# Six-block attention and two gated layers on one core: how the second block's probabilities are normalised and transposed, how two biases and merged weight bits are formed, and an order that knows of an exclusion between two engines

## The chip, the cores and the metric

The kernel runs on one core of one Trainium2 chip. The number is device microseconds from the start to the end of one execution. An engine is named as the profile names it: PE (TensorE, matmuls; PEld is its weight load), DVE (VectorE), ACT (ScalarE), POOL (GpSimd), SP (SyncE, which here issues most DMAs). PSUM is the memory that PE writes, in 8 banks of 128 x 512 fp32 numbers; SBUF is the working memory.

## The reference

```python
# q, k, v: 4 x 8 x 576 x 64, fp32
scores = scale * q @ k^T                       # per batch and head, 576 x 576
kth = the 32nd largest of each row
scores = where(scores >= kth, scores, -1e9)
attn = exp(scores - max) / (sum + 1e-9)
x = (attn @ v) laid out as 2304 x 512
h = x @ w_in ;  x = (h * sigmoid(h)) @ w_out   # w_in 512 x 2048, w_out 2048 x 512
out = (((x @ w1) * (x @ w2)) @ w3) @ w_out2    # w1, w2 512 x 1024, w3 1024 x 1024, w_out2 1024 x 512
```

## The kernel before

The weights arrive as 64-bit floats, read as pairs of 32-bit words. The 2304 tokens are worked in six blocks of 384 (`BLOCKS`), each three tiles of 128 rows for each of 8 heads. While the dense layers of block j run on PE (`mlp`), the attention of block j + 1 runs on the other engines and in PE's gaps. Block 0's attention has no dense layer to run beside; in its place the product of w3 and w_out2 is formed (`fold_steps`). The dense layers of block 0 run together with the conversion of the 48 pieces of w_in, w_out, w1 and w2 (`conv_step`), which later blocks read back from DRAM.

**Scores and top-k** (`plan_scores`, `plan_topk`). Two tiles make a pair; a block has 12 pairs. For each tile DVE finds the 32 largest of 576 scores with four MAX8 and three MATCH_REPLACE8. The eight-number results go into `tops`, which has a zero column in front and one behind, so that one subtraction of two strided columns (`bias`) gives both `nb` numbers of both tiles: minus the largest and minus the 32nd. ACT then masks (`mask`, with the 32nd) and takes the exponential (`ex`, with the largest), summing it. `recip` forms `rc`, one over the sum.

**Normalising and transposing** (`norm`, `plan_av`). In blocks 0 and 1 (`NATIVE`) the identity times `rc` is written as `dg` (by ACT for the first four pairs, by POOL after that), and an fp32 matmul of the unnormalised `e` with `dg` transposes and normalises at once, in five chunks of each tile. In blocks 2 to 5 POOL multiplies `e` itself by `rc`, and PE's transpose with the identity follows.

**Conversion of a weight piece.** `convert_load` brings 128 x 512 pairs into `raw`. `convert_scale`: ACT scales the high words into `t`; the low words are reduced to their top three bits, by ACT (`low` is the bias of that step) or, for even pieces from the eighth on (`LOWV`), by a DVE shift, in both cases back into `raw`; POOL clamps `t`. `convert_bits`: for the conversion a DVE SCALAR_TENSOR_TENSOR shifts `t` left by three and merges the low bits (`w<-t,raw`); for the fold (`MERGE`) DVE shifts and POOL adds. Then ACT rounds `w` into the first half of `wt` and POOL subtracts for the second.

**Order.** Every instruction is first recorded (`Recorder`); `schedule` then runs through them with costs of its own (`Op.cost`) and sets the order of each engine's queue, which is fixed in the program. Every recorded instruction has the line of the call in `emit`, so rows are told apart by their tiles. All PSUM tiles share one pool of 8 buffers (`bank`).

## Time and profile before

| | |
|---|---|
| median of 3 runs | 1153.53 us (1153.19 to 1156.3) |
| the profiled execution | 1153.59 us, its span from first to last instruction 1151.8 us |
| busy over the span | PE 95%, PEld 87%, DVE 81%, ACT 74%, POOL 65% |
| last matmul of the fold | starts at 142.2 us |
| first matmul of block 0's dense layers | starts at 172.7 us |
| merges of the 48 pieces | start from 148.2 to 368.8 us |

A profile row gives the engine, the operation, its output and input tiles, the shapes, a count, the busy time and the mean of one. Idle time stands behind the second bar, with what ended it. L328 is the line in `emit` from which all recorded instructions are issued.

### The profile page before, as it was taken

The page shows a single profiled execution, that of the slowest core. Times are in us where ns is not written, and L with a number is a line of the kernel's source. Part 1 is how long each engine was busy: PE and PEld are TensorE (multiplying, and loading weights), DVE is VectorE, ACT ScalarE, POOL GpSimd, SP SyncE. Part 2 cuts the span into 40 slices and gives each one's busy share as a digit, 9 for nine tenths or more (in the row PEclk, how much of TensorE's full clock was granted, in tenths as well). Part 3 has the DMA queues.
Part 4 walks back from the last instruction along what each step waited for, and adds up shares of the span by engine and source line. Part 5 has one row for each costly group of instructions (what it writes and reads, how often), then busy time and mean ns, then how long its engine had stood idle before and what let it go on. Part 6 is the DMA issues. An engine that isn't in the chain of part 4 may idle for free.

```text
span 1151.8 us, 19674 instructions
## 1 busy us (share of the span) xinstructions
PE 1097.8 (95%) x6216; PEld 998.5 (87%) x6216; DVE 927.7 (81%) x1990; ACT 854.6 (74%) x1911; POOL 744.0 (65%) x767
## 2 busy tenths in 40 slices
PE   4889987989999999999999999999999999999998
PEld 3555566979898999999999998999999999999997
DVE  7999899999979899999999997898899999501100
ACT  6988699879887688888888877877878788642221
POOL 4678368887876476777777866776766577542221
PEclk9999988999999999999999999999999999999999
DMA  8886278898989677675888667898766766348840
GB/s 250 282 271 197 92 256 281 311 310 317 313 267 316 201 237 235 216 240 183 276 268 276 216 225 242 268 321 291 241 212 230 249 217 221 127 154 259 253 152 28
DMA packets 127879, 273.54 MB, mean 237 GB/s; under 512 B 40480, under 2 KB 65056, under 8 KB 127776
## 3 DMA queue, kind: packets, MB, share of 16 engines
q1 hardware_dynamic: 119712, 245.02, 65.7%
q10 hardware_dynamic: 8064, 27.27, 6.0%
q8 instruction: 50, 0.82, 0.3%
q14 instruction: 53, 0.43, 0.1%
HBM read 216.14 MB, written 56.10 MB: 236 GB/s over the span
## 4 chain that ended last, share of the span: by engine, by line
PE 58%; DVE 21%; ACT 8%; POOL 6%; issue 5%; DMA 2%; ACTq 0%; SPq 0%; POOLq 0%; DVEq 0%
PE bank L328 58%; DVE tops L328 9%; DVE wk L328 7%; DVE w L328 2%; ACT e L328 2%; POOL wt L328 2%; POOL gl L328 1%; DMA kk<-k 1%; DVE gf L328 1%; ACT st L328 1%; POOL t L328 1%; DVE nb L328 1%; ACT wt L328 1%; ACT t L328 1%; DMA scr<-wt 1%
## 5 line engine op out<-in xcount | busy, mean ns | idle before, releaser
L328 DVE MAX8 tops<-wk 128x8 f32<-128x576 f32 x432 | 320.5, 753 | 5.7
L328 POOL TENSOR_TENSOR gl<-gf,gh 128x384 fp32r<-128x384 f32 x144 | 148.8, 1033 | 162.8 <-ACT gh L328 161.7
L328 PE MATMUL bank<-gh,wt 128*128 128x384 f32 x768 | 225.9, 344 | 7.3 <-ACT gh L328 7.1
L328 PE MATMUL bank<-xh,wt 128*128 128x384 f32 x768 | 223.2, 341 | 0.3 <-ACT st L328 0.2
L328 PE MATMUL bank<-x2h,wt 128*128 128x384 f32 x768 | 219.7, 341 | 0.1
L328 DVE MATCH_REPLACE8 wk<-tops,wk 128x576 f32<-128x576 f32 x288 | 213.2, 741 | 0.0
L328 PE MATMUL bank<-kk,qs 128*128 128x288 f32 x640 | 149.5, 320 | 16.0 <-ACT kk L328 13.2
L328 ACT ACTIVATE st<-bank 128x288 f32<-128x288 f32 (+1 forms) x320 | 129.0, 410 | 38.0 <-PE bank L328 33.4
L328 POOL TENSOR_TENSOR pl<-pf,ph 128x384 fp32r<-128x384 f32 x128 | 129.7, 1021 | 37.9 <-ACT ph L328 36.1
L328 PEld LDWEIGHTS bank<-gh,wt 128*128 128x128 f32 x768 | 141.2, 189 | 9.0 <-ACT gh L328 8.3
L328 PEld LDWEIGHTS bank<-kk,qs 128*128 128x128 f32 x640 | 116.0, 194 | 34.7 <-issue 16.5
L328 PEld LDWEIGHTS bank<-xh,wt 128*128 128x128 f32 x768 | 141.6, 189 | 2.4 <-issue 0.8
L328 PEld LDWEIGHTS bank<-x2h,wt 128*128 128x128 f32 x768 | 140.7, 188 | 2.7 <-DVE gf L328 0.5
L328 PE MATMUL bank<-gl,wt 128*128 128x384 f32 x384 | 131.3, 342 | 3.8 <-POOL gl L328 3.4
L328 DVE MAX8 tops<-st 128x8 f32<-128x576 f32 x144 | 107.6, 751 | 32.4 <-ACT st L328 31.9
L328 PE MATMUL bank<-x2l,wt 128*128 128x384 f32 x384 | 129.0, 337 | 0.5 <-POOL x2l L328 0.4
L328 PE MATMUL bank<-xl,wt 128*128 128x384 f32 x384 | 129.3, 337 | 0.1
L328 ACT ACTIVATE e<-st,nb 128x576 f32<-128x576 f32 x144 | 107.7, 777 | 19.5 <-DVE nb L328 18.2
L328 ACT CAST gh<-gf 128x384 fp32r<-128x384 f32 x144 | 74.0, 514 | 60.4 <-DVE gf L328 58.1
L328 ACT ACTIVATE e<-e,nb 128x576 f32<-128x576 f32 x144 | 111.3, 775 | 0.5 <-POOL wt L328 0.5
L328 DVE SCALAR_TENSOR_TENSOR gf<-th,bank 128x384 f32<-128x384 f32 x96 | 52.3, 545 | 68.8 <-ACT th L328 66.9
L328 DVE MATCH_REPLACE8 wk<-tops,st 128x576 f32<-128x576 f32 x144 | 106.5, 741 | 0.0
(80 smaller groups left out, 2374.5 us busy)
## 6 DMA issues: line engine op xcount, KB each, us to landing
wt<-scr SPq DMA_DIRECT2D x240, 512.0 KB, 4.2
scr<-wt ACTq DMA_DIRECT2D x48, 512.0 KB, 5.7
k<-kk SPq DMA_DIRECT2D x32, 576.0 KB, 4.5
kk<-k SPq DMA_DIRECT2D x32, 576.0 KB, 5.2
raw<-in_w_dram SPq DMA_DIRECT2D x24, 512.0 KB, 5.5
kr<-in_kT_dram SPq DMA_DIRECT2D x32, 288.0 KB, 5.0
raw<-in_w3T_dram SPq DMA_DIRECT2D x16, 512.0 KB, 5.0
raw<-in_w_in_dram SPq DMA_DIRECT2D x16, 512.0 KB, 5.2
```

The costliest lines, as they stand in the source:

```text
L328: o.call(*[real_ap(x) for x in o.args], **{k: real_ap(x) for k, x in o.kw.items()})
```

## The change

The change has four parts. Block 1 (`NATIVE` but not `DIAG`) lets POOL multiply `e` by `rc` and transposes with the identity; block 0 keeps `dg`. The biases are formed by two TENSOR_REDUCE with one input each, in place of one subtraction with two inputs, and `tops` becomes a tile `top` of a pool. For the 28 of 48 pieces whose low bits ACT forms, ACT writes them to a PSUM bank (`LOWP`), so that the merge reads one input from PSUM. And `schedule` holds a DVE instruction that `port` marks as sharing back while a POOL instruction runs by its costs, and the other way round; if POOL is busy for more than `AVOID` ns, a ready DVE instruction that does not share goes first.

```diff
+AVOID = 60
+DIAG = lambda j: j == 0
+LOWP = lambda n: n >= 0
...
+    def port(self):
+        if self.engine != "vector" or self.name in ("max", "match_replace", "tensor_reduce", "reciprocal"):
+            return False
+        return not in_bank(self.ins)
...
             if self.name == "tensor_scalar":
-                t = 850 if src.dtype == I16 else max(360, n * 1.14 + 45)
+                t = 740 if src.dtype == I16 else max(360, n * 1.14 + 45)
...
+            late = 0.
+            if o.shares and busy > t + AVOID:
+                aside = [n]
+                while ready[e] and ops[ready[e][0]].shares:
+                    aside.append(heapq.heappop(ready[e]))
+                n = heapq.heappop(ready[e]) if ready[e] else aside.pop(0)
+                for x in aside:
+                    heapq.heappush(ready[e], x)
+                o = ops[n]
+            if o.shares:
+                late = max(0., busy - t)
+                held = t + late + o.hold
+            elif e == "gpsimd":
+                late = max(0., held - t)
+                busy = t + late + o.hold
...
         if LOWV(n):
-            nc.vector.tensor_scalar(r[:, :, 0], r[:, :, 0], 29, None, op0=ALU.logical_shift_right)
+            u = r[:, :, 0]
+            nc.vector.tensor_scalar(u, u, 29, None, op0=ALU.logical_shift_right)
         else:
-            nc.scalar.activation(out=r[:, :, 0].bitcast(I32), in_=r[:, :, 0], func=ACTF.Identity,
+            u = bank("low") if LOWP(n) else r[:, :, 0].bitcast(FP32)
+            nc.scalar.activation(out=u.bitcast(I32), in_=r[:, :, 0], func=ACTF.Identity,
                                  bias=low, scale=2.0 ** -29 * (1.0 - 2.0 ** -16))
...
-            nc.vector.scalar_tensor_tensor(out=w.bitcast(U32), in0=t.bitcast(U32), scalar=3, in1=r[:, :, 0],
+            nc.vector.scalar_tensor_tensor(out=w.bitcast(U32), in0=t.bitcast(U32), scalar=3, in1=u,
...
         def bias():
             t = st["top"]
-            nc.vector.tensor_sub(out=st["nb"][:, 0:m], in0=t[:, 0:m, TOPK:TOPK + 2], in1=t[:, 0:m, 1:TOPK + 1:TOPK - 1])
+            nc.vector.tensor_reduce(out=t[:, 0:m, TOPK:TOPK + 2], in_=t[:, 0:m, 0:TOPK:TOPK - 1].unsqueeze(3), axis=AX, op=ALU.add, negate=True)
+            nc.vector.tensor_reduce(out=st["nb"][:, 0:m], in_=t[:, 0:m, TOPK - 1:TOPK + 1], axis=AX, op=ALU.add)
...
-            if NATIVE(j):
+            if NATIVE(j) and not DIAG(j):
+                x = p = e[:, 0:S]
+            elif NATIVE(j):
...
-                        nc.tensor.matmul(ps[0:kn, i * 128:(i + 1) * 128], lhsT=p[:, kc * 128:kc * 128 + kn],
-                                         rhs=st["d"][:, i * 128:(i + 1) * 128], start=True, stop=True)
+                        if DIAG(j):
+                            nc.tensor.matmul(ps[0:kn, i * 128:(i + 1) * 128], lhsT=p[:, kc * 128:kc * 128 + kn],
+                                             rhs=st["d"][:, i * 128:(i + 1) * 128], start=True, stop=True)
+                        else:
+                            nc.tensor.transpose(ps[0:kn, i * 128:(i + 1) * 128], p[:, kc * 128:kc * 128 + kn], ident)
```

The queue of DVE at the end of the first pair of block 0, before (`w<-t` is a shift of the fold, `st` a pair's scores, `wk` what is left of them):

```order
L328 MATCH_REPLACE wk<-tops,wk 128x576 x2
L328 TENSOR_SCALAR w<-t 128x512
L328 MAX tops<-wk 128x8 x2
L328 TENSOR_SCALAR w<-t 128x512
L328 TENSOR_TENSOR nb<-tops 128x4
L328 MAX tops<-st 128x8
L328 MATCH_REPLACE wk<-tops,st 128x576
L328 MAX tops<-st 128x8
```

and in the changed program:

```order
L356 MATCH_REPLACE wk<-top,wk 128x576 x2
L356 TENSOR_SCALAR w<-t 128x512
L356 MAX top<-wk 128x8 x2
L356 MAX top<-st 128x8
L356 TENSOR_REDUCE top<-top 128x2x2
L356 TENSOR_SCALAR w<-t 128x512
L356 TENSOR_REDUCE nb<-top 128x2
L356 MAX top<-st 128x8
L356 MATCH_REPLACE wk<-top,st 128x576 x2
```

The first maximum of the next pair has moved ahead of the bias, which now stands as two rows with a fold shift between them.

The queue of DVE in block 0's dense layers from their second gate on, before (`raw<-raw` is a DVE shift of low bits, `gf` the gate of a dense layer):

```order
L328 SCALAR_TENSOR_TENSOR gf<-th,bank 128x384
L328 MATCH_REPLACE wk<-tops,wk 128x576 x2
L328 MAX tops<-wk 128x8 x2
L328 TENSOR_SCALAR raw<-raw 128x512
L328 TENSOR_TENSOR nb<-tops 128x4
L328 MAX tops<-st 128x8
L328 SCALAR_TENSOR_TENSOR w<-t,raw 128x512
L328 MAX tops<-st 128x8
L328 MATCH_REPLACE wk<-tops,st 128x576
L328 SCALAR_TENSOR_TENSOR gf<-th,bank 128x384
L328 MATCH_REPLACE wk<-tops,st 128x576
L328 SCALAR_TENSOR_TENSOR w<-t,raw 128x512
```

and in the changed program, again from the second gate on (`w<-t,bank` is a merge with its low bits in PSUM):

```order
L356 SCALAR_TENSOR_TENSOR gf<-th,bank 128x384
L356 TENSOR_REDUCE top<-top 128x2x2
L356 MAX top<-st 128x8
L356 TENSOR_REDUCE nb<-top 128x2
L356 TENSOR_SCALAR raw<-raw 128x512
L356 MATCH_REPLACE wk<-top,st 128x576
L356 MAX top<-st 128x8
L356 SCALAR_TENSOR_TENSOR w<-t,raw 128x512
L356 MATCH_REPLACE wk<-top,st 128x576
L356 MAX top<-wk 128x8 x2
L356 SCALAR_TENSOR_TENSOR w<-t,bank 128x512
L356 TENSOR_SCALAR raw<-raw 128x512
```

The gate has moved behind two matches and two maxima that used to follow it, and the shift of low bits and the merge from SBUF each stand some rows later among the maxima. At the thirteenth gate 28 merges and 160 maxima stood ahead, and now 29 and 160: the places move, the proportion does not.

The queue of POOL at the first tiles of block 1, before (`t` is the clamp, `wt` the second half of a weight piece, `kk` and `qs` the splits of keys and queries):

```order
L328 TENSOR_SCALAR dg<-ident,rc 128x128 x2
L328 TENSOR_TENSOR kk<-kr,kk 128x576
L328 TENSOR_TENSOR xl<-xf,xh 128x384
L328 TENSOR_SCALAR t<-t 128x512
L328 TENSOR_TENSOR wt<-w,wt 128x512
L328 TENSOR_SCALAR dg<-ident,rc 128x128
L328 TENSOR_SCALAR t<-t 128x512
L328 TENSOR_TENSOR wt<-w,wt 128x512
L328 TENSOR_SCALAR t<-t 128x512
L328 TENSOR_TENSOR wt<-w,wt 128x512
L328 TENSOR_SCALAR dg<-ident,rc 128x128
```

and in the changed program:

```order
L356 TENSOR_SCALAR e<-e,rc 128x576 x2
L356 TENSOR_TENSOR kk<-kr,kk 128x576
L356 TENSOR_TENSOR xl<-xf,xh 128x384
L356 TENSOR_SCALAR t<-t 128x512
L356 TENSOR_TENSOR wt<-w,wt 128x512
L356 TENSOR_SCALAR t<-t 128x512
L356 TENSOR_SCALAR e<-e,rc 128x576
L356 TENSOR_TENSOR wt<-w,wt 128x512
L356 TENSOR_SCALAR t<-t 128x512
L356 TENSOR_TENSOR wt<-w,wt 128x512
L356 TENSOR_SCALAR e<-e,rc 128x576
```

Where `dg` stood, the multiplication of `e` stands, with one clamp moved ahead of it. No DMA is added or taken away on any queue.

## Rows read from the trace of the kernel before

**Rows 1.** Windows by stage: busy us of PE, PEld, DVE, ACT, POOL; clock; DMA share.

```profile
...
0.00:150.00 150.00, 125.97 (x502) 76.14 (x503) 138.24 (x298) 117.97 (x253) 91.08 (x100) 1.00 0.68 215
150.00:372.00 222.00, 201.12 (x1137) 180.64 (x1135) 207.58 (x406) 189.74 (x400) 171.09 (x168) 0.96 0.88 300
372.00:1152.00 780.00, 770.72 (x4582) 741.75 (x4581) 581.90 (x1288) 546.87 (x1260) 481.79 (x500) 1.00 0.68 224
```

**Rows 2.** Chain that ended last, by line: 0 to 150 us, then 150 to 372 us.

```profile
...
by line: DVE tops L328 37.9%; DVE wk L328 30.0%; DVE w L328 8.6%; PE bank L328 6.8%; issue 4.5%; DMA raw<-in_w_dram 3.9%; DVE nb L328 3.1%; ACT st L328 1.1%; DVE rc L328 0.9%; ACT t L328 0.8%; SPq L328 0.5%; ACT e L328 0.5%; ACT raw L328 0.
...
by line: PE bank L328 20.9%; POOL wt L328 8.1%; issue 7.3%; DVE w L328 7.0%; ACT e L328 6.6%; DMA kk<-k 5.9%; DVE tops L328 5.1%; POOL t L328 4.7%; DVE wk L328 4.4%; ACT wt L328 3.7%; ACT t L328 3.3%; DMA scr<-wt 3.0%; POOL gl L328 2.7%; AC
...
```

**Rows 3.** DVE groups, 0 to 150 us: count, busy us, mean ns, idle before.

```profile
...
L328 DVE TENSOR_SCALAR w<-t 128x512 uint32<-128x512 uint32 x24 | 15.1, 630 | 0.0
L328 DVE TENSOR_TENSOR nb<-tops 128x4 f32<-128x4 f32 x11 | 5.3, 486 | 0.0
...
L328 DVE TENSOR_TENSOR kk<-kr,kk 128x576 fp32r<-128x576 f32 x1 | 0.8, 759 | 0.5 <-ACT kk L328 0.5
```

**Rows 4.** DVE groups, 150 to 372 us, same columns.

```profile
...
L328 DVE SCALAR_TENSOR_TENSOR w<-t,raw 128x512 uint32<-128x512 uint32 x47 | 44.5, 947 | 7.6 <-POOL t L328 7.6
...
L328 DVE TENSOR_SCALAR raw<-raw 128x512 uint32<-128x512 uint32 x20 | 13.4, 669 | 0.0
L328 DVE TENSOR_TENSOR nb<-tops 128x4 f32<-128x4 f32 x14 | 8.9, 636 | 0.0
```

**Rows 5.** Tile views of w, raw, nb, rc, gf: ns min/median/max, first and last start.

```profile
...
L328 DVE SCALAR_TENSOR_TENSOR w<-t,raw x48: 662/836/1942, 148.2 to 368.8; 128x512 uint32<-128x512 uint32 x48
...
L328 DVE TENSOR_SCALAR w<-t x24: 398/414/1297, 17.2 to 122.8; 128x512 uint32<-128x512 uint32 x24
...
L328 DVE TENSOR_SCALAR raw<-raw x20: 403/560/1507, 187.0 to 362.7; 128x512 uint32<-128x512 uint32 x20
...
L328 DVE TENSOR_TENSOR nb<-tops x72: 140/342/1251, 19.8 to 993.9; 128x4 f32<-128x4 f32 x72
...
L328 DVE TENSOR_REDUCE rc<-sums x72: 129/146/158, 25.6 to 997.6; 128x2 f32<-128x4 f32 x72
...
L328 DVE SCALAR_TENSOR_TENSOR gf<-th,bank x96: 524/544/556, 183.8 to 1092.1; 128x384 f32<-128x384 f32 x96
```

**Rows 6.** Timelines of POOL and DVE near 176 us: start us, duration us, what.

```profile
...
176.13 1.44 POOL L328 TENSOR_TENSOR kk<-kr,kk 128x576 fp32r<-128x576 f32 x1
177.52 1.47 POOL L328 TENSOR_TENSOR xl<-xf,xh 128x384 fp32r<-128x384 f32 x1
...
176.17 1.94 DVE L328 SCALAR_TENSOR_TENSOR w<-t,raw 128x512 uint32<-128x512 uint32 x1
178.04 0.98 DVE L328 TENSOR_TENSOR nb<-tops 128x4 f32<-128x4 f32 x1
```

**Rows 7.** PE groups over the span: block 0 and 1 (dg), blocks 2 to 5 (ident).

```profile
...
L328 PE MATMUL bank<-ident,e 128*128 128x128 f32 x480 | 78.1, 272 | 0.0
L328 PE MATMUL bank<-dg,e 128*128 128x128 f32 x384 | 59.9, 290 | 12.8 <-POOL dg L328 6.3 <-ACT st L328 3.1 <-ACT dg L328 1.7
...
L328 PE MATMUL bank<-dg,e 128*64 128x128 f32 x96 | 14.1, 281 | 0.0
```

**Rows 8.** POOL groups: dg in 150 to 372 us, e over the span.

```profile
...
L328 POOL TENSOR_SCALAR dg<-ident,rc 128x128 f32<-128x128 f32 x26 | 11.6, 453 | 10.5 <-DVE rc L328 9.6
...
L328 POOL TENSOR_SCALAR e<-e,rc 128x640 f32<-128x640 f32 x96 | 76.8, 808 | 30.3 <-DVE rc L328 25.6 <-ACT st L328 3.8
```

**Rows 9.** Two windows of 20 us in the second stage, same columns as rows 1.

```profile
...
160.00:180.00 20.00, 16.88 (x78) 13.48 (x79) 19.90 (x40) 18.10 (x39) 12.76 (x15) 0.83 0.70 242
180.00:200.00 20.00, 13.29 (x76) 12.38 (x75) 20.00 (x39) 17.53 (x37) 16.27 (x16) 0.83 0.92 312
```

**Rows 10.** Timelines of ACT and DVE near 151 us.

```profile
...
150.42 0.74 ACT L328 ACTIVATE raw<-raw,low 128x512 int32<-128x512 uint32 x1
...
152.66 0.67 DVE L328 SCALAR_TENSOR_TENSOR w<-t,raw 128x512 uint32<-128x512 uint32 x1
```

More of the change, by code (lines that the diff above doesn't have):

```diff
@@ L107, in real_ap, with in_bank @@
     return ap
+def in_bank(aps):
+    return any(isinstance(x, View) and x.tile.key[1] == "bank" for x in aps)
 def columns(ap):
@@ L144, in __init__ @@
         self.hold, self.done = self.cost()
+        self.shares = self.port()
+    def port(self):
+        if self.engine != "vector" or self.name in ("max", "match_replace", "tensor_reduce", "reciprocal"):
+            return False
+        return not in_bank(self.ins)
     def cost(self):
@@ L167, in cost @@
                 if src.dtype == U32:
-                    t = 850 if len(self.ins) > 1 else n / 1.92 + 62
+                    t = n / 1.92 + 65 if len(self.ins) == 1 else t
             return t, t + 98
@@ L262, in schedule @@
         free = dict.fromkeys(ready, 0.)
-        wire = 0.
+        wire = busy = held = 0.
         reserved = {}
@@ L301, in schedule @@
             o = ops[n]
+            late = 0.
[13 more added lines that the diff above has]
+                busy = t + late + o.hold
             start[n] = t
-            free[e] = t + o.hold
-            end = t + o.done
+            free[e] = t + late + o.hold
+            end = t + late + o.done
             if o.dma:
@@ L386, in attention_moe_moe2_kernel @@
     sums = w4_p.tile([128, 4, 2, 2], FP32, name="sums")
-    tops = w4_p.tile([128, 2, 2, TOPK + 2], FP32, name="tops")
     def convert_load(ap):
@@ L400, in convert_scale, with convert_bits @@
         if LOWV(n):
-            nc.vector.tensor_scalar(r[:, :, 0], r[:, :, 0], 29, None, op0=ALU.logical_shift_right)
-        else:
-            nc.scalar.activation(out=r[:, :, 0].bitcast(I32), in_=r[:, :, 0], func=ACTF.Identity,
+            u = r[:, :, 0]
+            nc.vector.tensor_scalar(u, u, 29, None, op0=ALU.logical_shift_right)
+        else:
+            u = bank("low") if LOWP(n) else r[:, :, 0].bitcast(FP32)
+            nc.scalar.activation(out=u.bitcast(I32), in_=r[:, :, 0], func=ACTF.Identity,
                                  bias=low, scale=2.0 ** -29 * (1.0 - 2.0 ** -16))
+            u = u.bitcast(U32)
         top = t.bitcast(I16).rearrange("p (f t) -> p f t", t=2)[:, :, 1]
         nc.gpsimd.tensor_scalar(top, top, 32767, FLOOR, op0=ALU.min, op1=ALU.max)
-        return t
-    def convert_bits(r, t, n=-1):
+        return t, u
+    def convert_bits(t, u, n=-1):
         w = raw_p.tile([128, 512], FP32, tag="w", bufs=WB, name="w")
@@ L412, in convert_bits @@
             nc.vector.tensor_scalar(w.bitcast(U32), t.bitcast(U32), 3, None, op0=ALU.logical_shift_left)
-            nc.gpsimd.tensor_tensor(out=w.bitcast(I32), in0=w.bitcast(I32), in1=r[:, :, 0].bitcast(I32), op=ALU.add)
+            nc.gpsimd.tensor_tensor(out=w.bitcast(I32), in0=w.bitcast(I32), in1=u.bitcast(I32), op=ALU.add)
         else:
-            nc.vector.scalar_tensor_tensor(out=w.bitcast(U32), in0=t.bitcast(U32), scalar=3, in1=r[:, :, 0],
+            nc.vector.scalar_tensor_tensor(out=w.bitcast(U32), in0=t.bitcast(U32), scalar=3, in1=u,
                                            op0=ALU.logical_shift_left, op1=ALU.bitwise_or)
@@ L452, in conv_step @@
         if 0 <= a < NH:
-            conv_st[a] = (conv_st[a], convert_scale(conv_st[a], a))
+            conv_st[a] = convert_scale(conv_st[a], a)
         a = k - 3
@@ L517, in step @@
             if 0 <= a < len(jobs):
-                st[a] = (st[a], convert_scale(st[a]))
+                st[a] = convert_scale(st[a])
             a = k - 3
@@ L699, in begin @@
         def begin():
-            st["top"] = tops[:, n % 2]
-            st["nb"] = s_p.tile([128, 2, 2], FP32, tag="nb", name="nb")
+            st["top"] = s_p.tile([128, 2, TOPK + 2], FP32, tag="top", name="top")
+            st["nb"] = s_p.tile([128, 2], FP32, tag="nb", name="nb")
             st["sm"] = sums[:, n % 4]
@@ L709, in mx @@
             for i in range(m):
-                nc.vector.max(out=st["top"][:, i, r * 8 + 1:r * 8 + 9], in_=st["s" if r == 0 else "wk"][:, i])
+                nc.vector.max(out=st["top"][:, i, r * 8:r * 8 + 8], in_=st["s" if r == 0 else "wk"][:, i])
         def mr(r):
             for i in range(m):
-                nc.vector.match_replace(out=st["wk"][:, i], in_to_replace=st["top"][:, i, r * 8 + 1:r * 8 + 9],
+                nc.vector.match_replace(out=st["wk"][:, i], in_to_replace=st["top"][:, i, r * 8:r * 8 + 8],
                                         in_values=st["s" if r == 0 else "wk"][:, i], imm_value=-3.0e38)
@@ L726, in mask @@
                 nc.scalar.activation(out=e[:, 0:S], in_=st["s"][:, i], func=ACTF.Prelu,
-                                     bias=st["nb"][:, i, 1:2], alpha=BELOW)
+                                     bias=st["top"][:, i, TOPK + 1:TOPK + 2], alpha=BELOW)
         def ex():
@@ L731, in ex @@
                 e = st["e"][i][:, 0:S]
-                nc.scalar.activation(out=e, in_=e, func=ACTF.Exp, bias=st["nb"][:, i, 0:1],
+                nc.scalar.activation(out=e, in_=e, func=ACTF.Exp, bias=st["nb"][:, i:i + 1],
                                      accum_out=st["sm"][:, i, 0:1])
@@ L1096, in attention_moe_moe2_kernel @@
         real.gpsimd.memset(sums, 1e-9)
-        real.gpsimd.memset(tops, 0.0)
         real.gpsimd.memset(low, 7.5 * 2.0 ** -16 - 0.5)
```

## The prediction

> **What bounds the kernel now.** I first read the busy time of the engines by stage. The borders are my choice, at the start of block 0's dense layers and at the last converted weight piece. In the first stage (0 to 150 us) DVE is busy 138.2 of 150 us. In the second (150 to 372 us) DVE has 207.6 of 222, PE 201.1, ACT 189.7, POOL 171.1, and the DMA engines a share of 0.88. In the third (372 us to the end) PE has 770.7 of 780, and DVE only 581.9 [rows 1]. The reader should see three bounds: DVE; a crowd led by DVE; PE.
>
> The chain that ended last says the same. In the first stage the maxima, matches, fold shifts and biases of DVE hold 37.9 + 30.0 + 8.6 + 3.1 = 79.6% of it. In the second no engine holds it: PE has 20.9%, the merges on DVE 7.0% [rows 2]. So what DVE saves in the first stage arrives whole, in the second in part, and in the third not at all, as DVE has 198 us to spare there.
>
> Third, how DVE's time is spent. A merge from SBUF takes from 662 to 1942 ns, a fold shift 398 to 1297, a shift of low bits 403 to 1507, a bias 140 to 1251. Two other kinds hardly vary: the small reduction for `rc` takes 129 to 158 ns, the gate with one input in PSUM 524 to 556 [rows 5]. The timelines show why. A merge starts at 176.17 us, just after POOL began a subtraction that ends at 177.57; the merge ends at 178.11, so 0.54 us after it. The bias behind it ends at 179.02, when POOL's next one ends at 178.99 [rows 6]. The varying kinds wait for the POOL instruction in flight, the steady ones do not.
>
> The Trainium skill, page "SBUF — State Buffer", section "SBUF: two separate sides", gives the rule: one pair of ports is shared by the two engines, whoever starts first holds it for the whole instruction, and of DVE's instructions only those with two SBUF inputs or in a two-port mode need it. The timeline agrees. The rule also speaks against this change, since a longer POOL instruction holds the pair longer; by rows that is priced below with POOL's part.
>
> **The biases.** A bias takes a mean of 486 ns in the first stage (11 of them) [rows 3] and 636 in the second (14) [rows 4]. Two reductions stand in its place. Their shape has no row; the nearest is the reduction for `rc`, median 146 [rows 5], so I take 292 for both. That gives 11 x (486 - 292) = 2.1 us and 14 x (636 - 292) = 4.8 us. At 158 each it is 1.9 and 4.5; if the second hides behind the instruction between them, 3.7 and 6.9. The mask waits for the first reduction and the exponential for the second, each up to one maximum later than now; the DVE queue has the next pair in it meanwhile, so I cost that at nothing in these stages.
>
> **The merges with a PSUM input.** 28 of 48 merges change, 27 of them in the second stage. None of this shape has a row. The gate with 384 columns takes 544, and 128 columns more cost 128 x (759 - 140) / 572 = 139 by the subtractions of 576 and 4 columns [rows 3, 5], together 683. Against the mean of 947 [rows 4] that is 27 x 264 = 7.1 us. If PSUM cost nothing more than SBUF alone (662) it is 7.7, and nothing if such merges waited as before, which the gate's narrow spread speaks against. ACT's write to PSUM has no row either; its write to SBUF takes 0.74 us [rows 10], and a fifth more on 28 of them would be 4 us, hidden in ACT's 32 idle us of the second stage. I take nothing.
>
> **The order.** 24 fold shifts lose 24 x (630 - 398) = 5.6 us [rows 3, 5]; the 20 merges and 20 shifts of low bits that stay in SBUF lose 20 x (947 - 662) + 20 x (669 - 403) = 11.0 us [rows 4, 5]. The new order is made from a list of costs and is fixed; on the chip the two queues drift against each other by more than one instruction, so it can meet a free POOL or miss it. I take a third, 2.0 and 3.5 us. All of it is one end; the other is as much lost again.
>
> **Block 1 on PE.** The 240 fp32 matmuls with `dg` (480 records) take 59.9 + 14.1 = 74.0 us, 308 ns each; the 480 transposes of blocks 2 to 5 take 78.1, 163 each [rows 7]. 120 of them change: 120 x 145 = 17.4 us less in the second stage, from 201.1 to 183.7. What follows a transpose, the copy from PSUM, stays.
>
> **Block 1 on POOL.** 24 products of 453 ns [rows 8] become 24 of 576 columns; the same step with 640 takes 808, so 727 by its columns. That is 24 x 274 = 6.6 us more, for a POOL of 171.1 in 222, with the clamps and the weights' second halves queued behind it. DVE's remaining SBUF instructions meet a POOL that is busy 80% of the time and not 77%, which takes about 0.4 us of their 11; I neglect it.
>
> **The sum.** First stage: 2.1 + 2.0 = 4.1 us, all on the chain. Second stage: DVE loses 4.8 + 7.1 + 3.5 = 15.4 of its 207.6. Two readings of what arrives: by load, if DVE's 14.4 idle us stay, the stage shrinks by all 15.4, to 206.6, with ACT at 189.7 and DMA at 0.88 x 222 = 195 still under it. By the chain, the merges hold 7.0% of 222 = 15.5 us, of which 27/47 are spared 264/947, so 2.5; PE holds 46.4 us, of which 17.4/201.1 go, 4.0; together 6.5, with biases and shifts that the row cuts off to come. I take 10, between the two, since DVE is the nearest to full but the chain changes engines too often to follow it alone. Third stage: nothing. 4.1 + 10 = 14.1 us off the profiled execution's 1153.59 gives 1139.5; the median, 1153.53, is the same to a tenth.
>
> **Rivals.**
> *Slower, by PSUM.* Each of the 28 low-bit tiles holds one of eight banks from ACT's write to the end of the merge: 150.42 to 153.33, so 2.9 us, where POOL is not in the way [rows 10]. If PE, whose next tile needs that bank, waits 1 us each time, 28 us are added and 1167 results; from 0.5 us on average the gain is gone. Against it: 28 x 2.9 = 81 bank-us of 8 x 222 = 1776 is 5%, and PE has 21 idle us in the stage. Chance 0.13.
> *Hardly a change.* DVE's relief in the second stage is taken up by waits for ACT and DMA, the fuller engines after the change; the first stage's 2 to 4 us remain: 1150 to 1152. For it: the chain changes engines often there [rows 2]. Chance 0.13.
> *Much faster.* The order frees all locked time and it all arrives: 2.1 + 5.6 + 4.8 + 7.1 + 11.0 = 30.6 us, 1123. Against it: the fixed order. Chance 0.08.
> *The clock.* The second stage has a mean granted clock of 0.96 [rows 1], from stretches at 1.2 GHz like those in the two windows at 0.83, where PE was busy 16.9 and 13.3 of 20 us [rows 9]: 0.04 x 2 x 222 = 17.8 us at the lower level. Block 1 gives PE less to do, so there may be more of them. Twice as many cost PE 8.9 us; it would have 192.6 of work, less than now, and half of the 8.9 landing gives 1144. Against it: the third stage holds 480 transposes at 1.00. Chance 0.08.
> The Trainium skill, page "TensorE: Matmul & The Clock Gate", section "Part 4: PE-mode transpose", speaks for this one: the full clock does not engage for transposes. The third stage's 1.00 does not bear it out where other matmuls stand between them.
>
> **Chances and range.** A measurement of this kernel tells some 0.3%, 3.5 us, from no change. The forecast, 6 to 23 us less, has 0.58; its own range is 1130 to 1147. Faster by over 0.3%: 0.58 + 0.08 + 0.08, and 0.04 of the second rival: 0.78. Within: its other 0.09. Slower: 0.13. From 1126 to 1153 leaves out the first rival and part of the third, under 0.2.
>
> **What the profile will show.** In the second stage the merges from `bank` all near 680 ns whatever POOL does; the reductions for the biases near 146; the rest of the merges and shifts with means between today's and their minima; PE's records with `ident` grown by 120 and with `dg` halved; the products with `e` near 727. Block 0's dense layers should start some 4 us earlier, the third stage some 14, at an unchanged length. The prediction is wrong if PE or ACT show waits on `w` at PSUM tiles, if the clock in the second stage falls below 0.96, or if the third stage's length changes.

## The result, and the profile after

The changed kernel takes 1140.01 us (median of 4 runs, 1139.82 to 1140.21), the kernel before 1154.27 in the same session: a ratio of 0.987 with an interval of 0.9853 to 0.9887, so 14.3 us less. The profiled execution of the changed kernel took 1139.82 us, with a span of 1138.0. All recorded instructions now have the line L356.

The windows by stage of the changed kernel, with the columns and the first two borders of [rows 1]:

```profile
0.00:150.00 150.00, 125.52 (x516) 76.97 (x517) 136.34 (x321) 123.10 (x264) 93.94 (x103) 0.95 0.72 224
150.00:372.00 222.00, 197.35 (x1079) 179.00 (x1079) 199.97 (x432) 192.16 (x406) 172.56 (x168) 0.95 0.89 304
372.00:1138.00 766.00, 758.16 (x4505) 730.95 (x4503) 566.90 (x1312) 539.61 (x1242) 478.81 (x496) 1.00 0.69 225
```

Borders at fixed times mix what moved with what changed. Two events are better borders: the first matmul of block 0's dense layers, and the first output copy of block 0, which ends the crowded stage. They are the first starts in the tile views of `xh` and `o`. Of the kernel before:

```profile
L328 PE MATMUL bank<-xh,wt x768: 332/334/689, 172.7 to 1091.1; 128*128 128x384 f32 x192
...
L328 ACT COPY o<-bank x18: 575/587/594, 390.4 to 1148.3; 128x512 f32<-128x512 f32 x18
```

and of the changed kernel:

```profile
L356 PE MATMUL bank<-xh,wt x768: 331/334/689, 165.7 to 1077.2; 128*128 128x384 f32 x192
...
L356 ACT COPY o<-bank x18: 582/588/596, 378.1 to 1134.5; 128x512 f32<-128x512 f32 x18
```

So the first stage is 7.0 us shorter (172.7 to 165.7), the second 5.3 (217.7 to 212.4), and the third 1.5 (1151.8 - 390.4 = 761.4, and 1138.0 - 378.1 = 759.9). The windows between these events, of the kernel before:

```profile
172.70:390.40 217.70, 201.82 (x1164) 184.79 (x1164) 201.13 (x398) 179.37 (x380) 167.23 (x165) 0.98 0.86 293
```

and of the changed kernel:

```profile
165.70:378.10 212.40, 191.23 (x1047) 175.62 (x1047) 190.26 (x411) 179.63 (x381) 169.28 (x164) 0.94 0.88 300
```

Between these borders PE and DVE were equally full before, 201.8 and 201.1 of 217.7, and both have lost eleven microseconds. The stage has lost half of that.

The chain that ended last, by line, 0 to 150 us and then 150 to 372 us of the changed kernel:

```profile
by line: PE bank L356 62.9%; DVE top L356 10.8%; DVE wk L356 8.7%; DMA raw<-in_w_dram 3.9%; DVE w L356 2.4%; DMA vn<-in_v_dram 1.8%; ACT e L356 1.6%; issue 1.5%; ACT t L356 1.2%; ACT st L356 1.1%; ACT pn L356 1.1%; ACT bank L356 0.8%; SPq L
...
by line: PE bank L356 48.7%; ACT e L356 5.5%; issue 4.7%; DVE top L356 4.5%; DVE wk L356 3.9%; ACT t L356 3.3%; ACT wt L356 2.7%; POOL wt L356 2.7%; DMA kk<-k 2.4%; ACT bank L356 2.2%; ACT st L356 2.2%; ACT pn L356 2.1%; DMA wt<-scr 2.1%; P
```

Where DVE held 79.6% of the first stage's chain and PE 20.9% of the second's [rows 2], PE now holds 62.9% and 48.7%. The first of these is mostly one piece, from 69.27 us on, which lasts 71.51 us and has 280 matmuls:

```profile
69.27 71.51 PE bank L356 x280
```

So from 69 to 141 us PE, and no longer DVE, is on this chain: DVE's relief has brought PE to the front in the first stage too.

The tile views of the changed kernel, in the form of [rows 5]:

```profile
L356 DVE SCALAR_TENSOR_TENSOR w<-t,bank x28: 659/676/690, 142.4 to 354.4; 128x512 uint32<-128x512 uint32 x28
L356 DVE TENSOR_SCALAR w<-t x24: 397/416/1181, 17.1 to 118.7; 128x512 uint32<-128x512 uint32 x24
...
L356 DVE SCALAR_TENSOR_TENSOR w<-t,raw x20: 668/748/1516, 185.0 to 355.0; 128x512 uint32<-128x512 uint32 x20
...
L356 ACT ACTIVATE bank<-raw,low x28: 707/731/760, 140.4 to 351.8; 128x512 int32<-128x512 uint32 x28
...
L356 DVE TENSOR_SCALAR raw<-raw x20: 414/574/1416, 182.8 to 354.1; 128x512 uint32<-128x512 uint32 x20
...
L356 DVE TENSOR_REDUCE nb<-top x72: 127/148/161, 20.3 to 980.0; 128x2 f32<-128x4 f32 x72
...
L356 POOL TENSOR_SCALAR e<-e,rc x120: 746/805/1086, 168.8 to 984.8; 128x640 f32<-128x640 f32 x96, 128x576 f32<-128x576 f32 x24
```

Merges with an input in PSUM lie within 31 ns of each other; merges from SBUF still spread over 850. The timelines show both kinds against POOL, as in [rows 6] (start, duration, what). POOL's:

```profile
202.76 1.29 POOL L356 TENSOR_TENSOR wt<-w,wt 128x512 fp32r<-128x512 f32 x1
...
213.04 1.36 POOL L356 TENSOR_TENSOR wt<-w,wt 128x512 fp32r<-128x512 f32 x1
```

and DVE's:

```profile
203.34 0.67 DVE L356 SCALAR_TENSOR_TENSOR w<-t,bank 128x512 uint32<-128x512 uint32 x1
...
213.77 1.18 DVE L356 SCALAR_TENSOR_TENSOR w<-t,raw 128x512 uint32<-128x512 uint32 x1
```

At 203.34 a merge with PSUM runs inside POOL's 1.29 us and takes 0.67. At 213.77 a merge from SBUF meets a POOL instruction that ends at 214.40, and ends 0.55 us after it.

### The profile page after: what moved, and what is told of

The parts are those of the page before. It is cut to its first block, busy times and chain, and to the rows that moved or that the text cites. A ratio compares the mean times of both kernels' runs of the same rounds, so it can differ in the third digit from the quotient of the medians.

```text
span 1138.0 us, 19557 instructions
## 1 busy us (share of the span) xinstructions
PE 1081.0 (95%) x6096; PEld 986.9 (87%) x6096; DVE 903.2 (79%) x2062; ACT 854.9 (75%) x1911; POOL 745.3 (65%) x766
## 4 chain that ended last, share of the span: by engine, by line
PE 79%; ACT 7%; DVE 6%; POOL 3%; issue 3%; DMA 2%; ACTq 0%; SPq 0%; POOLq 0%; DVEq 0%
PE bank L356 79%; DVE top L356 3%; DVE wk L356 2%; ACT e L356 2%; POOL gl L356 1%; ACT t L356 1%; ACT st L356 1%; DVE w L356 1%; ACT wt L356 1%; ACT bank L356 1%; POOL wt L356 1%; ACT pn L356 1%; DMA raw<-in_w_dram 1%; DMA kk<-k 0%; DMA wt<-scr 0%
## 5 line engine op out<-in xcount | busy, mean ns | idle before, releaser
L356 DVE MAX8 top<-wk 128x8 f32<-128x576 f32 x432 | 319.9, 753 | 5.3
L356 POOL TENSOR_TENSOR gl<-gf,gh 128x384 fp32r<-128x384 f32 x144 | 147.2, 1022 | 158.8 <-ACT gh L356 157.6
L356 PE MATMUL bank<-xh,wt 128*128 128x384 f32 x768 | 225.0, 344 | 7.7 <-ACT st L356 7.0
L356 PE MATMUL bank<-gh,wt 128*128 128x384 f32 x768 | 224.9, 343 | 3.7 <-ACT gh L356 3.5
L356 PE MATMUL bank<-x2h,wt 128*128 128x384 f32 x768 | 221.7, 344 | 0.2 <-ACT x2h L356 0.2
L356 DVE MATCH_REPLACE8 wk<-top,wk 128x576 f32<-128x576 f32 x288 | 213.3, 742 | 0.0
L356 PE MATMUL bank<-kk,qs 128*128 128x288 f32 x640 | 150.8, 322 | 21.8 <-ACT kk L356 15.2
L356 ACT ACTIVATE st<-bank 128x288 f32<-128x288 f32 (+1 forms) x320 | 129.3, 411 | 39.8 <-PE bank L356 36.7
L356 POOL TENSOR_TENSOR pl<-pf,ph 128x384 fp32r<-128x384 f32 x128 | 129.5, 1018 | 38.0 <-ACT ph L356 35.8
L356 PEld LDWEIGHTS bank<-kk,qs 128*128 128x128 f32 x640 | 116.3, 195 | 41.1 <-issue 18.6
L356 PEld LDWEIGHTS bank<-xh,wt 128*128 128x128 f32 x768 | 142.9, 190 | 10.1 <-ACT st L356 7.7
L356 PEld LDWEIGHTS bank<-gh,wt 128*128 128x128 f32 x768 | 141.4, 190 | 5.1 <-ACT gh L356 4.7
L356 PEld LDWEIGHTS bank<-x2h,wt 128*128 128x128 f32 x768 | 141.6, 189 | 2.6 <-ACT x2h L356 0.8
L356 PE MATMUL bank<-gl,wt 128*128 128x384 f32 x384 | 131.4, 342 | 2.4 <-POOL gl L356 1.9
L356 DVE MAX8 top<-st 128x8 f32<-128x576 f32 x144 | 108.0, 752 | 29.2 <-ACT st L356 28.4
L356 PE MATMUL bank<-xl,wt 128*128 128x384 f32 x384 | 130.5, 340 | 0.0
L356 PE MATMUL bank<-x2l,wt 128*128 128x384 f32 x384 | 129.9, 339 | 0.1
L356 POOL TENSOR_SCALAR e<-e,rc 128x640 f32<-128x640 f32 (+1 forms) x120 | 95.6, 805 | 35.5 <-DVE rc L356 32.9
L356 ACT CAST gh<-gf 128x384 fp32r<-128x384 f32 x144 | 74.1, 515 | 52.7 <-DVE gf L356 51.5
L356 ACT ACTIVATE e<-st,top 128x576 f32<-128x576 f32 x144 | 107.4, 778 | 6.6 <-DVE top L356 5.3
L356 ACT ACTIVATE e<-e,nb 128x576 f32<-128x576 f32 x144 | 111.6, 777 | 0.0
L356 DVE SCALAR_TENSOR_TENSOR gf<-th,bank 128x384 f32<-128x384 f32 x96 | 52.5, 547 | 74.2 <-ACT th L356 72.5
```

Of the source, the lines that this page charges most:

```text
L356: o.call(*[real_ap(x) for x in o.args], **{k: real_ap(x) for k, x in o.kw.items()})
```

## The experiments

Three theories stood at first. **Load**: DVE bounds the first stage and leads the second, so each part brings what it spares DVE, whole in the first stage and about two thirds in the second, and the parts add. **PE**: the gain comes from block 1's cheaper transposes. **Order**: it comes from the new order, whatever the instructions. A fourth, **neighbours**, was formed after the first four runs and is first called "load theory, second form": the engines stand right behind each other in the second stage, so a part that relieves one brings little until the others are relieved with it. Beside them stood the rivals on record (waits for PSUM banks, the clock). "Order" means the order list of the queues, which is made anew whenever the recorded instructions or their costs change.

### Each part alone, added to the kernel before

The edits are parts of the diff above; their cores, in the order of the runs:

```diff
+LOWP = lambda n: n >= 0
...
+            u = bank("low") if LOWP(n) else r[:, :, 0].bitcast(FP32)
```

> The kernel before with the PSUM merges alone: 28 merges near 680 ns, the other 20 as before. Load theory (what DVE is relieved of arrives, whole in the first stage and about two thirds in the second): 0.3 + 7.1 x 2/3 = 5 us faster, near 1149. PE theory (the gain comes from block 1's cheaper transposes): no change. Order theory (the gain comes from the new order, whatever the instructions): a few us either way. PSUM rival: slower, because PE waits for banks.

```diff
+            nc.vector.tensor_reduce(out=t[:, 0:m, TOPK:TOPK + 2], in_=t[:, 0:m, 0:TOPK:TOPK - 1].unsqueeze(3), axis=AX, op=ALU.add, negate=True)
+            nc.vector.tensor_reduce(out=st["nb"][:, 0:m], in_=t[:, 0:m, TOPK - 1:TOPK + 1], axis=AX, op=ALU.add)
```

> The kernel before with the two one-input reductions alone: both near 146 ns. Load theory: 2.1 + 4.8 x 2/3 = 5 us faster, near 1149. PE theory: no change in the second stage, so 2 us at most. Order theory: a few us either way.

```diff
+            if NATIVE(j) and not DIAG(j):
+                x = p = e[:, 0:S]
...
+                            nc.tensor.transpose(ps[0:kn, i * 128:(i + 1) * 128], p[:, kc * 128:kc * 128 + kn], ident)
```

> The kernel before with block 1's POOL product and transposes alone: 17 us less PE work in the second stage, 7 us more on POOL, DVE as it was. Load theory: DVE sets the stage, so within 4 us of before, 1150 to 1154. PE theory: the stage shortens by most of it, 10 us or more, under 1144.

```diff
+            if o.shares and busy > t + AVOID:
+                aside = [n]
...
-                t = 850 if src.dtype == I16 else max(360, n * 1.14 + 45)
+                t = 740 if src.dtype == I16 else max(360, n * 1.14 + 45)
```

> The kernel before with the order that knows of the exclusion, and no other change. Load theory: only what the means of fold shifts, merges and shifts of low bits fall: 2 to 5 us faster, 1149 to 1152, with the fold shifts under 500 ns. Order theory: most of the 14 us, under 1145.

Measured against 1154.9 us: `psum_alone` 1156.27 us, ratio 1.0012 (0.9999 to 1.0024); `bias_alone` 1155.83, 1.0005 (0.9993 to 1.0017); `block1_alone` 1153.72, 0.9986 (0.9974 to 0.9998); `order_alone` 1154.01, 0.999 (0.9978 to 1.0001). No part alone is worth more than block 1's 0.14%, whose interval ends just under 1, and the four add to -0.07%, against -1.3% together. The load theory falls by the merges and the biases, for which it had 5 us each. The PE theory had block 1 alone under 1144, and the order theory the order alone under 1145; both fall.

### Each part left out of the changed kernel

```diff
-        return not in_bank(self.ins)
+        return False
...
-                    t = n / 1.92 + 65 if len(self.ins) == 1 else t
+                    t = n / 1.92 + 62 if len(self.ins) == 1 else t if in_bank(self.ins) else 850
...
-                t = 740 if src.dtype == I16 else max(360, n * 1.14 + 45)
+                t = 850 if src.dtype == I16 else max(360, n * 1.14 + 45)
```

> The changed kernel with the old order: no exclusion and the old costs in the list. None of the four parts alone gave more than 1.2 us, so the load theory in its first form has fallen. Fit theory (the order pays only where DVE's durations are what its list assumes, which the one-input reductions and PSUM merges make true): most of the 14 us are lost, 1149 or more. Load theory, second form (the parts relieve engines that stand just behind each other, so that only all together shorten the stage, the order being of no weight): within 4 us of the changed kernel, 1140 to 1144.

```diff
-DIAG = lambda j: j == 0
+DIAG = lambda j: j < 2
```

> The changed kernel with the matmuls by dg in block 1 again. Fit theory: POOL and PE steps of block 1 change no DVE duration, so 1 to 4 us lost at most, 1141 to 1144. Load theory, second form: PE with its 17 us more is again the engine just behind DVE, and most of the 14 us are lost, 1149 or more.

```diff
-            nc.vector.tensor_reduce(out=t[:, 0:m, TOPK:TOPK + 2], in_=t[:, 0:m, 0:TOPK:TOPK - 1].unsqueeze(3), axis=AX, op=ALU.add, negate=True)
-            nc.vector.tensor_reduce(out=st["nb"][:, 0:m], in_=t[:, 0:m, TOPK - 1:TOPK + 1], axis=AX, op=ALU.add)
+            nc.vector.tensor_sub(out=st["nb"][:, 0:m], in0=t[:, 0:m, TOPK:TOPK + 2], in1=t[:, 0:m, 1:TOPK + 1:TOPK - 1])
```

> The changed kernel with the one subtraction of two inputs for the biases again. Both theories: the first stage loses 2 to 3 us. Fit theory: another few us in the second stage, as the bias is again 140 to 1250 ns long against a list that shifts it aside: 1143 to 1148. Load theory, second form: most of the 14 us lost.

```diff
-LOWP = lambda n: n >= 0
+LOWP = lambda n: False
```

> The changed kernel with all low bits in SBUF again. Fit theory: the list still sets these merges aside from POOL's instructions, and part of the gain stays: 1143 to 1149. Load theory, second form: 7 us more on DVE, most of the 14 us lost, 1149 or more.

Measured against 1156.49 us: without the order 1144.38 us, 0.9896 (0.9877 to 0.9915); without block 1 1150.1, 0.9942 (0.9928 to 0.9957); without the biases 1149.76, 0.9938 (0.9922 to 0.9955); without the merges from PSUM 1150.99, 0.9952 (0.9937 to 0.9968). Against the 0.987 of the whole, leaving out the order loses 3 us (the intervals overlap), and leaving out any of the other three loses 8 to 10. The four losses add to 2.5%, twice the whole. The fit theory had most of the gain lost without the order, and at most 4 us lost without block 1; it falls. The neighbours' form had at most 4 us lost without the order and most of the gain lost without each other part, which is near what was measured. So these three seem to depend on each other; but each of the four kernels also has a new list, and the next runs show what that alone can do.

### The old order held

Each kernel so far has an order list made anew, so `bias_alone` is the biases and a new order, and the order theory had to be asked again: a **new list** may itself give or take what the parts seemed to. Next the old list was kept. The two reductions were recorded as one operation with the old one's cost; block 1's product and transposes were recorded in the places of the `dg` products and matmuls, with their costs (a `dg` tile that nothing reads stays allocated).

```diff
+            def both(out, accum_out, in0, in1):
+                real.vector.tensor_reduce(out=accum_out, in_=in0.unsqueeze(3), axis=AX, op=ALU.add, negate=True)
+                real.vector.tensor_reduce(out=out, in_=in1, axis=AX, op=ALU.add)
+
+            nc.add(Op("vector", both, "tensor_sub", (), dict(out=st["nb"][:, 0:m, 0], accum_out=t[:, 0:m, TOPK:TOPK + 2],
```

> The kernel before with the two one-input reductions, in exactly the order of before: where the subtraction stood on DVE the two reductions stand next to each other, and no other row of any engine moves. Rebuilt-order theory (each part is worth what the first sum said, and an order made anew for one part alone loses it again): 4 to 6 us faster, 1149 to 1151 if before is 1155. Neighbour theory (one engine's relief in the second stage is met by the next engine just behind): 2 to 3 us faster, the first stage's part, and nothing in the second.

```diff
+                def product(out, in0, rc, also, accum_out):
+                    real.gpsimd.tensor_scalar(also, also, rc, 1.0, op0=ALU.mult, op1=ALU.mult)
...
+                            def turn(out, lhsT, rhs, start, stop):
+                                real.tensor.transpose(out, lhsT, ident)
```

> The kernel before with block 1's product on POOL and transposes by the identity, in exactly the order of before, each in the place of the product with the identity and of the matmul with dg. Rebuilt-order theory: PE's chain share, about 4 us faster. Neighbour theory: under 2 us, as DVE's work is as before.

The third kernel has both edits.

> The kernel before with both of the last two edits, in exactly the order of before. Rebuilt-order theory: the sum of the two, 8 to 10 us. Neighbour theory: more than the sum of the two, as DVE and PE are relieved together, but most of the second stage's gain still waits for the PSUM merges: 4 to 7 us.

Measured against 1154.23 us: the biases 1148.41 us, 0.9951 (0.9936 to 0.9966); block 1 1160.24, 1.0047 (1.003 to 1.0064), slower; both 1154.93, 1.001 (0.9998 to 1.0023). Two things follow. In these two cases a new list shifted the time by half a per cent, once each way: by the ratios the biases are worth 0.0049 x 1154 = 5.7 us in the old order and nothing in a new one, and block 1 costs 5.4 in the old order and nothing in a new one. And in the old order the two edits add (-0.49% and +0.47%, together +0.10%); the neighbour theory wanted 4 to 7 us, more than the sum, and this pair speaks against it. The rebuilt-order theory is right on the biases alone (4 to 6 us), and wrong on block 1 (4 us faster) and on both (8 to 10).

The profile of `bias_in_old_order` does not show a gain in the second stage. That execution took 1150.15 us, the longest of its four; its span is 3.5 us shorter than before, 1.8 of it in the first stage and 1.8 in the third, and its second stage has 217.8 us for 217.7.

What the new order took from the biases shows in the waits of PE, 165 to 380 us (us in total, times, longest), of `bias_alone`:

```profile
PE bank L328 <- ACT gh L328: 16.9, 3, 6.5
```

and of `bias_in_old_order`:

```profile
PE bank L328 <- ACT gh L328: 7.5, 2, 4.3
```

In `bias_alone` PE's dense matmuls waited three times for ACT's rounding of the gates, 16.9 us in all; before it was 6.3. For block 1's edit, the POOL group of the product, 165 to 380 us of `block1_in_old_order` (count, busy us, mean ns):

```profile
L759 POOL TENSOR_SCALAR e<-e,rc 128x576 f32<-128x576 f32 x24 | 21.4, 900 | 8.0 <-DVE rc L328 7.1
```

and in two of its waits:

```profile
DVE w L328 <- POOL t L328: 11.4, 11, 4.0
...
PE bank L826 <- POOL e L759: 7.1, 9, 2.6
```

The same group and the same wait of PE in `block1_alone`, which has the edit and a new list:

```profile
L329 POOL TENSOR_SCALAR e<-e,rc 128x576 f32<-128x576 f32 x24 | 21.5, 900 | 2.1 <-DVE rc L329 0.5
...
PE bank L329 <- POOL e L329: 4.0, 3, 2.5
```

POOL spends 21.4 us on 24 products where 26 `dg` took 11.6 [rows 8], but 21.5 us in `block1_alone`, which loses nothing. So POOL's time is not what the old order adds. PE's waits are: 7.1 us for the products, 4.0 in `block1_alone` and 4.0 for `dg` before. DVE waits 11.4 us for POOL's clamps, 9.9 in `block1_alone` and 7.3 before. That is less than the 6 us between the two kernels; the rest was not traced.

### All merges from PSUM

The 20 shifts of low bits that stay on DVE write to a PSUM bank too, so all 48 merges read PSUM.

```diff
-            u = r[:, :, 0]
-            nc.vector.tensor_scalar(u, u, 29, None, op0=ALU.logical_shift_right)
+            u = bank("low").bitcast(U32)
+            nc.vector.tensor_scalar(u, r[:, :, 0], 29, None, op0=ALU.logical_shift_right)
```

> The changed kernel, in which the 20 shifts of low bits on DVE also write a PSUM bank, so that all 48 merges read PSUM; the order is made anew, with these shifts and merges as instructions that do not share. The shifts, one element at a time, near 600 ns for 696 now, the 20 merges near 680 for 926: 20 x (96 + 246) = 6.8 us less on DVE in the second stage. Neighbour theory: ACT and DMA are now the fuller engines, so 0 to 3 us faster than the changed kernel. PSUM rival: 20 more banks held among eight make PE wait, and it is slower than the changed kernel. Rebuilt-order theory: anything from 3 us faster to 5 us slower.

Measured: 1141.17 us, 0.9883 (0.9867 to 0.99), no better than the changed kernel. The tile views of its shifts and merges:

```profile
L356 DVE TENSOR_SCALAR bank<-raw x20: 674/685/696, 174.2 to 344.3; 128x512 uint32<-128x512 uint32 x20
...
L356 DVE SCALAR_TENSOR_TENSOR w<-t,bank x48: 667/678/690, 144.2 to 352.2; 128x512 uint32<-128x512 uint32 x48
```

All of DVE's merges are steady now, and the windows of the second stage of this kernel, between its own two events, say what that is worth:

```profile
167.60:379.20 211.60, 190.96 (x1044) 172.36 (x1044) 187.42 (x409) 179.38 (x382) 162.45 (x165) 0.95 0.88 302
```

DVE has 2.8 us less than in the changed kernel, where 6.8 was expected (the shifts take 685 ns, not 600), and POOL 6.8 less. The stage is 0.8 us shorter: PE's 191 is as it was, which on the reading of the next section leaves little to win from either. All 48 low-bit tiles hold a bank here, 20 more than in the change, and the time does not grow.

### The second stage of all kernels

For each kernel the windows between its first dense matmul and its first output copy were read as for the two above: where the stage begins, its length, the busy time of PE and DVE, and the length less the fuller of the two.

| kernel | begins | length | PE | DVE | length less the fuller |
|---|---|---|---|---|---|
| before | 172.7 | 217.7 | 201.8 | 201.1 | 15.9 |
| changed | 165.7 | 212.4 | 191.2 | 190.3 | 21.2 |
| `shift_to_psum` | 167.6 | 211.6 | 191.0 | 187.4 | 20.6 |
| `without_order` | 168.1 | 214.7 | 192.7 | 192.6 | 22.0 |
| `without_block1` | 166.4 | 220.1 | 202.2 | 191.2 | 17.9 |
| `without_bias` | 168.5 | 219.6 | 190.8 | 194.3 | 25.3 |
| `without_psum` | 169.0 | 222.1 | 191.7 | 195.8 | 26.3 |
| `psum_alone` | 171.4 | 222.6 | 202.5 | 193.5 | 20.1 |
| `bias_alone` | 170.1 | 224.2 | 201.6 | 199.7 | 22.6 |
| `block1_alone` | 172.7 | 219.4 | 191.5 | 204.0 | 15.4 |
| `order_alone` | 170.0 | 222.5 | 203.2 | 194.9 | 19.3 |
| `bias_in_old_order` | 170.9 | 217.8 | 203.2 | 197.8 | 14.6 |
| `block1_in_old_order` | 173.3 | 221.0 | 192.0 | 201.2 | 19.8 |
| `both_in_old_order` | 169.2 | 226.8 | 198.6 | 196.3 | 28.2 |

Each row is one execution. That of `both_in_old_order` lies 2.6 us above the median of its kernel and that of `block1_in_old_order` 2.7 below, so differences of 2 or 3 us between two rows say little.

What the table shows as it stands: the three kernels that have block 1's edit, the biases and the merges from PSUM, each with a list of its own, have 211.6 to 214.7 us, and the eleven that lack one of these have 217.7 or more.

The table also gives a new reading, formed after the runs and tested by none: in the second stage **PE and DVE are both the bound**, and here it is nowhere shorter than the fuller of them and some 15 us. Without block 1's edit PE keeps 201.6 to 203.2 us, whatever DVE is spared, and the stage takes 217.7 us or more. With it alone DVE keeps 201 to 204, and the stage takes 219 or more. Only where both fall to 193 and below is the stage under 215, in three kernels of three. What this reading leaves open is the last column, from 14.6 to 28.2 us: `without_bias` and `without_psum` lose 3 to 5 us by the fuller engine and 4 to 5 more there, and `both_in_old_order` gains 3 by its fuller engine and loses 12 there. And `bias_alone` has no more of either engine than the kernel before and takes 6.5 us longer, so the list weighs as much as an edit. How much of the last column is the order's luck was not separated; merges from PSUM were not tried in the old order, since their banks change the allocation.

In the first stage the parts look as if they add. To the first dense matmul the biases alone bring 2.6 us (1.8 in the old order), the order 2.7, the merges 1.3 and block 1 nothing, 6.6 together, against 7.0 measured. Left out, they lose 2.8, 2.4, 3.3 and 0.7, together 9.2; and `shift_to_psum`, whose first shift to PSUM starts at 174.2 us, begins its dense layers 1.9 us later than the changed kernel. So a list moves such a start by some 2 us, and adding is not shown.

## Why the prediction was right, point by point

The total was right, 14.1 us forecast and 13.8 between the profiled executions, with two of its terms wrong in opposite directions: 2.9 us too little in the first stage and 4.7 too much in the second. The third gave 1.5 where nothing was forecast. That these cancel to 0.3 us is luck.

**First stage: 4.1 us forecast, 7.0 measured.** In the changed kernel the mechanism held: what DVE is spared there arrives nearly whole. To the first dense matmul of the kernel before, and of the changed kernel:

```profile
0.00:172.70 172.70, 143.67 (x577) 88.45 (x577) 160.09 (x342) 138.59 (x297) 102.81 (x112) 0.98 0.70 225
...
0.00:165.70 165.70, 137.74 (x577) 85.33 (x577) 152.04 (x355) 138.32 (x296) 101.44 (x111) 0.96 0.74 235
```

DVE has 8.0 us less, and 7.0 arrive. It is no rule of this stage: `order_alone` spares DVE 6.2 us there and gains 2.7, `bias_alone` 4.7 and 2.6. The size was off twice. The prediction calls 150 us the start of the dense layers, which the table of before has at 172.7; that cut off 22.7 us in which DVE is busy for 21.9. The last matmul of the fold, at 142.2 us before and 137.5 after, had gained 4.7 of the 7.0. And the order recovered more than a third of the locked time of the fold shifts: a mean of 480 ns in place of 630 [rows 3], 24 x 150 = 3.6 us of 5.6, where I took 2.0 (a third is 1.9, and of the second stage's 11.0 it is 3.7, not 3.5). In the five other kernels with the exclusion in the schedule that mean is 478 to 506, in the four others with a new list 583 to 641. The DVE group of the changed kernel, 0 to 165 us:

```profile
L356 DVE TENSOR_SCALAR w<-t 128x512 uint32<-128x512 uint32 x24 | 11.4, 480 | 1.4 <-POOL t L356 1.2 <-issue 0.2
```

**Second stage: 10 us forecast, 5.3 measured.** The step that failed is the reading of "a crowd led by DVE". With borders at 150 and 372 us DVE had 207.6 and PE 201.1 [rows 1], and the sum took DVE as nearest to full; between the events the two are level, 201.1 and 201.8. So block 1's PE time, which the sum by load did not use, was not a term beside DVE's: on the reading above DVE's relief counts only with it, and the kernel without that edit has lost 8 of the 14 us. The fuller engine fell by 10.6 us, and 5.3 of them came back as time in which neither filled the stage.

The terms themselves: the biases 14 x (636 - 293) = 4.8 us, as forecast, by two reductions of 147 and 146 ns in these DVE groups (165 to 380 us):

```profile
L356 DVE SCALAR_TENSOR_TENSOR w<-t,raw 128x512 uint32<-128x512 uint32 x20 | 18.5, 926 | 1.0 <-POOL t L356 1.0
...
L356 DVE TENSOR_SCALAR raw<-raw 128x512 uint32<-128x512 uint32 x20 | 13.9, 696 | 0.0
L356 DVE TENSOR_REDUCE top<-top 128x4 f32<-128x4 f32 x14 | 2.1, 147 | 0.0
L356 DVE TENSOR_REDUCE nb<-top 128x2 f32<-128x4 f32 x14 | 2.0, 146 | 0.1
```

The merges with PSUM 676 where 683 stood. **The order's third is missing**: merges from SBUF have a mean of 926 and shifts of low bits 696, against 947 and 669 [rows 4], so 20 x 21 - 20 x 27 is about nothing where I took 3.5 us. `order_alone` shows it can be had (852 and 577 there), but PE then stays at 203.2.

**Block 1 on PE.** PE's groups over the span of the changed kernel:

```profile
L356 PE MATMUL bank<-ident,e 128*128 128x128 f32 x576 | 97.0, 275 | 5.6 <-POOL e L356 3.7 <-ACT pn L356 1.8
...
L356 PE MATMUL bank<-ident,e 128*64 128x128 f32 x24 | 4.3, 290 | 0.0
```

With the 27.2 + 7.0 us of `dg` that block 0 keeps, 135.5 us in place of 152.1 [rows 7]: 16.6 less, 17.4 forecast. But 3.4 of it are block 0's own `dg` (30.6 to 27.2 us in the first stage), which the edit does not touch. Between the two events, of the kernel before and of the changed one:

```profile
L328 PE MATMUL bank<-dg,e 128*128 128x128 f32 x192 | 29.3, 284 | 5.2 <-POOL dg L328 4.0 <-ACT a L328 0.6 <-ACT pn L328 0.4
...
L328 PE MATMUL bank<-dg,e 128*64 128x128 f32 x48 | 7.2, 282 | 0.0
...
L356 PE MATMUL bank<-ident,e 128*128 128x128 f32 x96 | 18.8, 290 | 5.6 <-POOL e L356 3.7 <-ACT pn L356 1.8
L356 PE MATMUL bank<-ident,e 128*64 128x128 f32 x24 | 4.3, 290 | 0.0
```

That is 36.5 to 23.1 us, 13.4 less: a transpose takes 192 ns here, where the forecast took the 163 of blocks 2 to 5. PE as a whole has 10.6 us less in the stage; the edit alone gives 10.3 (`block1_alone`), and leaving it out costs 11.0. (192 matmuls of 284 ns fill only 29.3 us, so they overlap, and the groups need not add up to the engine.) So PE's term was some 7 us too large; the sum used it only by its 4.0 us of the chain.

**Block 1 on POOL.** The product's mean is 800 ns, its minimum 746, where I had 727 by columns: POOL is held by DVE as DVE is by POOL. It is 8.3 us more and not 6.6. With the edit alone the mean is 900, in the old order and in a new one.

**Waits on PSUM banks** were to show in PE's waits on `w`. In the changed kernel, 165 to 380 us, there is one:

```profile
PE bank L356 <- DVE w L356: 0.3, 1, 0.3
```

PEld has one of 0.6 us. That rival is out, also by `shift_to_psum`, where PE's waits on `w` are 0.6 us. ACT's write to PSUM takes 731 ns and not more than to SBUF, as taken.

**The clock** did fall, as that rival said, without deciding. One of the signs that the prediction is wrong was a clock below 0.96 in the second stage; with its borders it reads 0.95, so that sign did show, by a hundredth. Between the events the granted clock went from 0.98 to 0.94: 0.02 x 2 x 217.7 = 9 us at 1.2 GHz before, 25 after. Part of that is the border: in the kernel before, 160 to 172.7 us has 0.73, but lies ahead of its second stage (see the first window of [rows 9]). In the changed kernel the slow stretch lies inside the stage; a window of 20 us reads:

```profile
180.00:200.00 20.00, 18.95 (x95) 18.34 (x96) 19.51 (x42) 17.46 (x37) 16.83 (x17) 0.78 0.87 301
```

The matmuls with `xh` have a mean of 371 ns in the second stage, 357 before (353 to 378 in the fourteen kernels). What the clock costs the stage was not tried. Over all fourteen kernels the granted clock between the two events is 0.92 to 0.96 in the eight with block 1's transposes, and 0.95 to 0.98 in the six without. The Trainium skill, page "TensorE: Matmul & The Clock Gate", section "Part 4: PE-mode transpose", says that the full clock does not engage for transposes; that difference goes with it, and the third stage, with most of blocks 2 to 5's 480 transposes at 1.00, does not. In the first stage the changed kernel has 0.95 for 1.00, and is 7 us shorter all the same. To their first dense matmul, where none has a transpose of block 1, the fourteen kernels have from 0.92 to 0.99, so differences of this size also come without these transposes; and that PE has less to do, the rival's own reason, was not told apart from them.

**Third stage**: 1.5 us shorter at a clock of 1.00, and 759.6 to 761.5 us in all fourteen kernels; "nothing", as forecast. The dense layers of block 0 start 7.0 us earlier, where some 4 were forecast, and the third stage 12.3, where some 14 were. The rival "hardly a change" named the right danger: 5.3 of 10.6 us did not arrive. The largest wait of PE that grew is for ACT's copies of scores, `st`: 7.0 us in the changed kernel between 165 and 380 us, 1.4 before. That this is where the relief went was not tried.

## What to carry to other kernels

Put the borders of stages at events (the first instruction of the next kind of work), not at round times: 22 us on the wrong side hid that two engines were level. Where two engines are level, an edit to one can measure as nothing alone and still be worth much among others: try them together, and leave them out one by one, before any is dropped. It is no law: in the old order the biases alone gave half a per cent, and with block 1's edit nothing. Where a scheduler makes the order anew for each edit, the new list alone was worth half a per cent here, once each way, so hold the order still when a single edit is to be priced.
